# Cosine-weighted linear attention into a two-layer MLP: where one block copies v, forms k^T v and loads k, and where the last block makes four sums of g

## The chip, the cores and the metric

One core of one Trainium2 chip runs the whole program in one launch. The metric is device time of an execution in microseconds (us), the median of repeated runs. Five engines work side by side and meet at semaphores: TensorE (PE, matmuls; PEld is its weight load), VectorE (DVE), ScalarE (ACT), GpSimd (POOL) and SyncE (SP, which here only issues DMAs). A transfer moves data between HBM and SBUF, or within SBUF with a transpose; matmuls write PSUM.

## The reference

Eight batches, 8 heads, 576 rows, head dimension 64. Attention has no softmax: relu of q and k is weighted by a cosine and a sine of the row's position, which doubles the feature dimension to 128.

```python
theta = np.pi / 2.0 * pos / S
q_p = concat([relu(q) * cos, relu(q) * sin], -1)      # phi
k_p = concat([relu(k) * cos, relu(k) * sin], -1)
kv = np.einsum('bhsf,bhsd->bhfd', k_p, v)
z = np.sum(k_p, axis=2)
num = np.einsum('bhsf,bhfd->bhsd', q_p, kv)
den = np.einsum('bhsf,bhf->bhs', q_p, z)[..., None] + 1e-06
x = (num / den), heads side by side: [4608, 512]
h = x @ w_in                                          # 512 -> 2048
g = h * sigmoid(1.702 * h)
out = g @ w_out                                       # 2048 -> 512
```

## The kernel before, in words

The work goes by batch, "block b" for short: 512 rows of it in the main stream, and its last 64 rows (the tails, gathered in `xt` and `gt`) in one go with those of the other batches at the end. While PE does the two products of block b, DVE, SP and PE prepare x of block nb = b + 1, and SP loads inputs of block b + 2.

What one block needs, in the names of the code:

- q' (`trig_q`, L176): ten DVE instructions make q' in `qn` from `qf`. Five DMA transposes on SP (`qturn_dma`, L217; "turns" below) put it into `qT`. Then `load_q` (L133) refills `qf` for two blocks on, by two DMAs.
- k' (`trig`, L161, called by `kv_operands`, L877): 18 DVE instructions from `kf` into `kr`. v is copied to bf16 by `vcopy` (L187) from `vf` into `vt`, which holds a column of ones that makes the sum z along with kv.
- k^T v (`kv_mm`, L232; `kv_mm_next`, L707): 72 small matmuls on PE into a PSUM tile "at" (there are two of these); `kv_evac` (L243) copies it to `kvs` on DVE. `kv_next` (L711) does both.
- x (`x_next`, L883), chunk by chunk (four of 128 rows and one of 64): `num_mm` (L304), 8 matmuls of `qT` by `kvs` into a tile "at"; `num_div` (L315), three DVE instructions (add of epsilon, reciprocal, multiply) into `xn`; `xturn_dma` (L351), a turn on SP into `xT`.
- First product (`mm1`, L373): 16 columns blocks fc of w_in, each 4 matmuls of 512 columns (L365) and one gelu on ACT (L371) into `gT`. mm1 of a block reads all four chunks of its `xT`.
- Second product (`wino_mm`, L508): a two by two block product by seven products instead of eight (the Winograd form), p1, p2, p6, p5, p7, p3, p4 in that order, each in two column halves c of 8 matmuls of 256 columns (L519). Step s = 2p + c counts the 14 halves. It needs sums of blocks of g, s1 to s4 (`g_sums`, L466; lines L473, L475, L477, L479), each in two halves h, on DVE: s2 for p6, s1 for p5, s3 for p7, s4 for p3. s2 needs s1, and s4 needs s2. p1, p2 and p4 read g itself. `wino_after` (L566) copies a finished product aside on ACT (`keep`, L527) or joins it with a kept one on DVE (`join`, L538), and POOL issues the output's DMA (L525).

Engines run their instructions in the order in which the code writes them: the order is written out by hand, under `manual_schedule`. SP's queue is served in that order too: an SP instruction that waits for its data holds all those behind it.

For block 1 (b == 1) the order around the change is: at fc 5 (the first four column blocks are in `start_block`, L715) q' of block 2 and its turns; at fc 6 k' of block 2, then the DMAs of q of batch 3; at fc 8 the two halves of s3; at fc 12 the first halves of s1 and s2; at fc 13 v's copy; then the second halves of s1 and s2; p1 (steps 0 and 1); k^T v and its copy, the first half of s4; p2 and so on, with chunks 0 to 4 of x after steps 3, 4, 5, 6 and 8, the second half of s4 after step 6, and the loads of k and v of batch 3 (`load_kv`, L146) on SP behind the turn of chunk 3. For blocks b > 1 k^T v comes at fc 14, chunk 0 of x ahead of the second product and the others in it, and k and v are loaded behind chunk 3 likewise.

The last block (L946 on) does the tails' first product (`mm1_tails`, L393, L396), and then splits the first product of its main rows by the Winograd form too (`Unit`, L642: `step` L674, matmuls L657, adds on DVE L666, copies on ACT L671, gelu L662). Between the steps of the units, `tail_half` (L967) puts in the 14 halves of the tails' second product. Its sums (`g_sums(..., TAIL)`) go into the space of `kr` (s1, s2) and `qT` (s3, s4); those of s3 and s4 stand behind the first half. Units 0 and 1 take turns in the PSUM banks, with `Bk` common to all units, so that step 2 of a unit writes the bank that the add of the unit before has read.

Of the kernel before, what the change touches and what calls it, by code (L numbers as in the profile page):

```python
# [20 lines left out]
def kernel(  # L21
# [9 lines left out]
    nc = tc.nc  # L31
# [25 lines left out]
    def src_of(src, b, i0=0, i1=NI):  # L57
        return src[b, 2 * i0:2 * i1].rearrange("(i hh) (p j) d -> (hh p) i (j d)", hh=2, j=NS)

    qf = one.tile([128, 2560], F32, name="qf")  # L60
    kf, vf = [one.tile([128, NI, S], F32, name=n) for n in ("kf", "vf")]
# [62 lines left out]
    def load(t, src, b, eng=nc.gpsimd):  # L124
        eng.dma_start(out=t, in_=src_of(src, b))

    def load_chunks(t, src, b, eng):
        eng.dma_start(out=t[:, 0:2048].rearrange("p (h e) -> p h e", h=H),
                      in_=src[b, :, 0:512, :].rearrange("h (p c) d -> p h (c d)", c=4))
        eng.dma_start(out=t[0:64, 2048:2560].rearrange("p (h e) -> p h e", h=H),  # L130
                      in_=src[b, :, 512:S, :].rearrange("h p d -> p h d"))

    def load_q(b, eng=nc.gpsimd):  # L133
        load_chunks(qf, q, b, eng)
# [11 lines left out]
    def load_kv(b):  # L146
        load(kf, k, b, nc.sync)
        load(vf, v, b, nc.sync)
# [27 lines left out]
    def trig_q(c, act=False):  # L176
        n = 128 if c < 4 else 64
        i = chunk(qf, c)
        for cs, w in enumerate((cosw, sinw)):
            o = qn[0:n, c, :, ts(cs, 64)]  # L180
            sc = w[0:n, NS + c:NS + c + 1]
            if act:
                nc.scalar.activation(o, i, AF.Relu, scale=sc)
            else:
                nc.vector.tensor_scalar(o, i, 0.0, sc, op0=MAX, op1=MUL)  # L185

    def vcopy(i0=0, i1=NI, act=False):  # L187
        o = vt[:, :, i0:i1, 0:64].rearrange("p j i e -> p i j e")
        i = vf[:, i0:i1].rearrange("p i (j e) -> p i j e", e=64)
        if act:  # L190
            nc.scalar.activation(o, i, AF.Copy)
        else:
            nc.vector.tensor_copy(o, i)  # L193
# [23 lines left out]
    def qturn_dma(c):  # L217
        n = 128 if c < 4 else 64
        nc.sync.dma_start_transpose(out=qT[:, :, c * 128:c * 128 + n],
                                    in_=qn[0:n, c].rearrange("p h f -> p (h f)"))  # L220
# [3 lines left out]
    def kv_open(i0=0, i1=NI, n=65):  # L224
        t = pat.tile([128, 2, 512], F32, name="at")
        for i in range(i0, i1):
            st["kv", i] = t[:, :, ds((i - i0) * n, n)]
        st["ps", i0] = t[:, :, 0:(i1 - i0) * n]
        if i0 == 0:
            st["kvs"] = small.tile([128, 2, NI, VW], BF16, name="kvs", bufs=2)  # L230

    def kv_mm(i0, i1, rhs, col, n):  # L232
        for i in range(i0, i1):
            for j in range(NS):
                for hh in range(2):
                    r = slice(hh * 64, hh * 64 + 64)
                    nc.tensor.matmul(st["kv", i][:, hh, ds(col, n)], kr[r, j, i, :], rhs(r, i, j),  # L237
                                     start=(j == 0), stop=(j == NS - 1))
# [4 lines left out]
    def kv_evac(i0, i1, n=65):  # L243
        o = st["kvs"][:, :, i0:i1, 0:n]
        nc.vector.tensor_copy(o, st["ps", i0].rearrange("p hh (i e) -> p hh i e", e=n))  # L245
# [58 lines left out]
    def num_mm(c, eps_too=False):  # L304
        ps = pat.tile([128, 2, 512], F32, name="at")
        if eps_too:
            for a in range(2):
                put_eps(ps[:, a])
        for h in range(H):
            nc.tensor.matmul(ps[:, h // 4, ds((h % 4) * 65, 65)], qT[:, h, ts(c, 128)],  # L310
                             kvs_of(h), start=not eps_too,
                             stop=(not eps_too or h % 4 == 3), skip_group_check=eps_too)
        nums[c] = [ps]

    def num_div(c, eps_too=False):  # L315
        ps = nums[c][0]
        pv = ps[:, :, 0:260].rearrange("p a (h e) -> p a h e", h=4)
        den = pv[:, :, :, 64]
        if not eps_too:
            den = small.tile([128, 2, 4], F32, name="den")  # L320
            nc.vector.tensor_scalar(den, pv[:, :, :, 64], 1e-6, None, op0=ADD)  # L321
        inv = small.tile([128, 2, 4], F32, name="inv")
        nc.vector.reciprocal(inv, den)  # L323
        xn = small.tile([128, 2, 4, 64], BF16, name="xn", bufs=5)
        nc.vector.tensor_tensor(xn, pv[:, :, :, 0:64],  # L325
                                inv.unsqueeze(3).to_broadcast([128, 2, 4, 64]), op=MUL)
        nums[c].append(xn)
# [23 lines left out]
    def xturn_dma(b, c):  # L351
        xn = nums.pop(c)[1]
        n = 128 if c < 4 else 64
        nc.sync.dma_start_transpose(out=x_cols(b, c),
                                    in_=xn[0:n].rearrange("p a h e -> p (a h e)"))
# [110 lines left out]
    def g_sums(names, h, of=MAIN):  # L466

        tt = nc.vector.tensor_tensor
        a_blk, to = of
        o = {n: to[n][:, ts(h, 4)] for n in to}  # L470
        for n in names:
            if n == "s1":
                tt(o[n], a_blk(1, h), a_blk(1, h + 2), op=ADD)  # L473
            elif n == "s2":
                tt(o[n], o["s1"], a_blk(0, h), op=SUB)  # L475
            elif n == "s3":
                tt(o[n], a_blk(0, h), a_blk(1, h), op=SUB)  # L477
            else:
                tt(o[n], a_blk(0, h + 2), o["s2"], op=SUB)  # L479
# [227 lines left out]
    def kv_mm_next():  # L707
        kv_open()
        kv_mm(0, 4, vt_rhs, 0, 65)

    def kv_next():  # L711
        kv_mm_next()
        kv_evac(0, 4)
# [163 lines left out]
    def kv_operands(b):  # L877
        for j in range(NS):
            trig(kr, kf, j)
        if b > 2:  # L880
            vcopy()

    def x_next(b, c):  # L883
        num_mm(c)
        num_div(c)
        xturn_dma(b, c)


    for b in range(1, B):
        nb = b + 1 if b + 1 < B else None  # L890
        if nb is None:
            break
        f0 = 5 if b == 1 else 0
        for fc in range(f0, FC):
            if nb is not None and fc == f0:
                for c in range(5):
                    trig_q(c)
                    qturn_dma(c)
            if nb is not None and fc == f0 + 1:
                kv_operands(nb)  # L900

                if nb + 1 < B:
                    load_q(nb + 1, nc.sync)
            if fc == 8 and b == 1:
                g_sums(("s3",), 0)
                g_sums(("s3",), 1)
            if fc == 12:
                if b > 1:
                    g_sums(("s3",), 0)
                    g_sums(("s3",), 1)  # L910
                g_sums(("s1", "s2", "s4") if b > 1 else ("s1", "s2"), 0)
            if fc == 13 and b == 1:
                vcopy()
            if fc == 14 and nb is not None and b > 1:
                kv_next()
            mm1(b, fc)
        if nb is not None:
            x_open(nb)
            if b > 1:
                x_next(nb, 0)  # L920
            g_sums(("s1", "s2"), 1)
            at = ({2 * p + 1: [p + 1 if nb < B - 1 else (4, 1, 2, 3)[p]] for p in range(4)} if b > 1 else
                  {3: [0], 4: [1], 5: [2], 6: [3], 8: [4]})
            wino_open()
            for p in range(7):
                for c in range(2):
                    wino_mm(p, c)
                    s = 2 * p + c
                    if c == 1:
                        wino_after(b, p)  # L930
                    for c2 in at.get(s, ()):
                        x_next(nb, c2)
                        if c2 == 3 and nb + 1 < B:
                            load_kv(nb + 1)
                    if s == 1 and b > 1:
                        g_sums(("s4",), 1)
                    if s == 1 and b == 1:
                        kv_mm_next()
                        kv_evac(0, 4)
                        g_sums(("s4",), 0)  # L940
                    if s == 6 and b == 1:
                        g_sums(("s4",), 1)
# [3 lines left out]
    b = B - 1  # L946
# [20 lines left out]
    def tail_half():  # L967
        p, c = next(halves)
        wino_mm(p, c, TAIL)
        if c == 1:  # L970
            wino_after(None, p, end=True)
        if (p, c) == (0, 0):
            for n in ("s3", "s4"):
                for h in range(2):
                    g_sums((n,), h, TAIL)
# [73 lines left out]
```

## Time and profile before

| | us |
|---|---|
| runs shown: median (lowest to highest of 3) | 277.95 (277.95 to 279.59) |
| the profiled execution | 280.04 |
| its span in the profile | 278.2 |
| PE busy | 269.8 |
| DVE busy | 199.3 |
| ACT busy | 133.9 |
| POOL busy | 41.3 |
| first matmul of mm1 in blocks 2, 3 and 4 at | 81.04, 110.90, 139.47 |

Times in the profile are counted from the start of the span. A row of the timeline gives start, length, engine, line, operation, tiles written and read, shapes and a count; in square brackets stand the engine's idle time ahead of it and what ended that. A length of a matmul group holds the drain of its last matmul, so the next group starts before it ends. Idle time of an engine that nothing waits for costs nothing. For a DMA, the row of SP tells how long SP took to issue it; when it landed is told separately ("to landing", counted from the start of the issue). The granted clock of PE is full (1.0) throughout.

### The profile page before, as it was taken

The page shows a single profiled execution, that of the slowest core. Times are in us where ns is not written, and L with a number is a line of the kernel's source. Part 1 is how long each engine was busy: PE and PEld are TensorE (multiplying, and loading weights), DVE is VectorE, ACT ScalarE, POOL GpSimd, SP SyncE. Part 2 cuts the span into 40 slices and gives each one's busy share as a digit, 9 for nine tenths or more (in the row PEclk, how much of TensorE's full clock was granted, in tenths as well). Part 3 has the DMA queues.
Part 4 walks back from the last instruction along what each step waited for, and adds up shares of the span by engine and source line. Part 5 has one row for each costly group of instructions (what it writes and reads, how often), then busy time and mean ns, then how long its engine had stood idle before and what let it go on. Part 6 is the DMA issues. An engine that isn't in the chain of part 4 may idle for free.

```text
span 278.2 us, 6718 instructions
## 1 busy us (share of the span) xinstructions
PE 269.8 (97%) x2748; PEld 195.1 (70%) x2748; DVE 199.3 (72%) x478; ACT 133.9 (48%) x237; POOL 41.3 (15%) x70
## 2 busy tenths in 40 slices
PE   7899999999999899999999999999999999999994
PEld 2585645856975488558855895589657976899984
DVE  4943776689885986987598759876987783654741
ACT  6967642674126511652166215621563147577621
POOL 5690000000130012100110022001200162000310
PEclk9999999999999999999999999999999999999999
DMA  7999999999699999996799969988993353000233
GB/s 232 253 211 298 275 286 155 260 296 191 189 138 374 169 210 216 351 170 176 197 335 170 202 168 371 189 191 110 356 252 32 88 165 119 0 2 0 79 112 113
DMA packets 73661, 53.57 MB, mean 193 GB/s; under 512 B 52736, under 2 KB 63488, under 8 KB 73632
## 3 DMA queue, kind: packets, MB, share of 16 engines
q1 hardware_dynamic: 67504, 36.97, 59.8%
q0 software_dynamic: 6128, 16.19, 21.2%
q8 instruction: 21, 0.34, 0.5%
q14 instruction: 8, 0.07, 0.1%
HBM read 36.70 MB, written 9.44 MB: 166 GB/s over the span
## 4 chain that ended last, share of the span: by engine, by line
PE 77%; DVE 10%; DMA 9%; SPq 1%; issue 1%; ACT 1%
PE mm L519 29%; PE mm L365 25%; DMA kf<-in_k_dram 9%; PE mm L396 4%; DVE kr L169 4%; PE mm L421 4%; PE mm L657 4%; PE at L519 3%; PE at L237 3%; PE at L310 3%; DVE vt L193 1%; DVE sums L477 1%; PE mm L205 1%; PE mm L388 1%; DVE sums L475 1%
## 5 line engine op out<-in xcount | busy, mean ns | idle before, releaser
L365 PE MATMUL mm<-xT,w_in 128*128 128x512 bf16 (+1 forms) x528 | 99.8, 345 | 0.0
L371 ACT ACTIVATE g<-mm 128x512 bf16<-128x512 f32 x112 | 66.0, 598 | 35.0 <-PE mm L365 35.0
L365 PEld LDWEIGHTS <-w_in 128*128 128x128 bf16 x528 | 53.0, 113 | 40.3
L519 PEld LDWEIGHTS <-sums 128*128 128x128 bf16 x448 | 42.4, 98 | 4.7
L525 POOL DMA_DIRECT2D out_dram<-ysb x24 | 17.4, 725 | 184.9 <-DVE inv L323 75.0
L519 PE MATMUL mm<-wsum,sums 128*128 128x256 bf16 x336 | 40.1, 272 | 0.0
L519 PEld LDWEIGHTS <-g 128*128 128x128 bf16 x336 | 32.1, 98 | 3.8
L169 DVE TENSOR_SCALAR kr<-kf,cosw 128x256 bf16<-128x256 f32 x69 | 24.4, 354 | 9.2 <-DMA kf<-in_k_dram 9.2
L325 DVE TENSOR_TENSOR xn<-at,inv 128x512 bf16<-128x512 f32 x39 | 27.0, 691 | 1.4
L519 PE MATMUL mm<-w_out_sb,g 128*128 128x256 bf16 x224 | 26.6, 273 | 0.0
L169 DVE TENSOR_SCALAR kr<-kf,sinw 128x256 bf16<-128x256 f32 x68 | 23.3, 342 | 0.0
L185 DVE TENSOR_SCALAR qn<-qf,cosw 128x512 bf16<-128x512 f32 (+1 forms) x33 | 16.4, 498 | 2.9 <-DMA qf<-in_q_dram 2.9
L534 ACT ACTIVATE kept_p<-mm 128x512 f32<-128x512 f32 (+1 forms) x15 | 8.5, 569 | 19.8 <-PE mm L519 19.8
L586 ACT ACTIVATE ysb<-mm 128x512 f32<-128x512 f32 x6 | 3.6, 598 | 29.0 <-PE mm L519 29.0
L310 PEld LDWEIGHTS <-qT 128*128 128x128 bf16 x312 | 14.3, 97 | 3.3 <-issue 1.0
L310 PE MATMUL at<-kvs,qT 128*128 128x65 bf16 x312 | 15.7, 193 | 0.8 <-DVE kvs L245 0.8
L321 DVE TENSOR_SCALAR den<-at 128x8 f32<-128x8 f32 x36 | 5.9, 163 | 14.7 <-PE at L310 14.6
L534 ACT ACTIVATE kept_u<-mm 128x512 f32<-128x512 f32 (+1 forms) x8 | 4.3, 544 | 24.9 <-DVE xn L325 16.8
L185 DVE TENSOR_SCALAR qn<-qf,sinw 128x512 bf16<-128x512 f32 (+1 forms) x33 | 15.7, 475 | 0.0
L421 PE MATMUL mm<-w_out_sb,g 128*128 128x512 bf16 x64 | 14.8, 379 | 0.0
L519 PE MATMUL mm<-w_out_sb,sums 128*128 128x256 bf16 x112 | 13.4, 273 | 0.0
L519 PE MATMUL mm<-wsum,g 128*128 128x256 bf16 x112 | 13.4, 272 | 0.0
(147 smaller groups left out, 320.2 us busy)
## 6 DMA issues: line engine op xcount, KB each, us to landing
kf<-in_k_dram SPq DMA_DIRECT2D x6, 1152.0 KB, 6.5
vf<-in_v_dram SPq DMA_DIRECT2D x6, 1152.0 KB, 11.2
qf<-in_q_dram SPq DMA_DIRECT2D x6, 1024.0 KB, 6.7
out_dram<-ysb POOLq DMA_DIRECT2D x24, 256.0 KB, 6.5
w_out_sb<-in_moe_w_out_dram POOLq DMA_DIRECT2D x4, 512.0 KB, 17.6
kf<-in_k_dram POOLq DMA_DIRECT2D x1, 1152.0 KB, 13.2
vf<-in_v_dram POOLq DMA_DIRECT2D x1, 1152.0 KB, 20.8
w_in<-in_moe_w_in_dram POOLq DMA_DIRECT2D x2, 512.0 KB, 10.0
```

What stands on the lines that cost most here:

```text
L169: eng.tensor_scalar(o, i, 0.0, w[:, j:j + 1], op0=MAX, op1=MUL)
L185: nc.vector.tensor_scalar(o, i, 0.0, sc, op0=MAX, op1=MUL)
L310: nc.tensor.matmul(ps[:, h // 4, ds((h % 4) * 65, 65)], qT[:, h, ts(c, 128)], kvs_of(h), start=not eps_too, stop=(not eps_too or h % 4 == ...
L325: nc.vector.tensor_tensor(xn, pv[:, :, :, 0:64], inv.unsqueeze(3).to_broadcast([128, 2, 4, 64]), op=MUL)
L365: nc.tensor.matmul(hp[fc][:, t0:t1], wcol(kc, fc), x[b][:, kc, t0:t1], start=(kc == 0), stop=(kc == KC - 1))
L371: nc.scalar.activation(gT[fc // 4][:, fc % 4], hp.pop(fc), AF.Gelu_apprx_sigmoid)
L396: nc.tensor.matmul(hps[:, 64:B * 64], wcol(kc, fc), xt[:, kc, 64:B * 64], start=(kc == 0), stop=(kc == KC - 1))
L421: nc.tensor.matmul(yp[b, t, c0][:, c0:c1], w, w_out_sb[:, fc, c0:c1], start=(fc == 0), stop=(fc == FC - 1))
L519: nc.tensor.matmul(bank[to][c], lhs, rhs, start=opens, stop=(fc == HF - 1), skip_group_check=True)
L525: eng.dma_start(out=dst[:, 2 * i + c0:2 * i + c1, ts(n, HD)], in_=t[:, c0:c1])
L534: nc.scalar.activation(o, i, AF.Identity)
L657: nc.tensor.matmul(to[:, j], lhs, rhs, start=(opens and j == 0 and k == 0), stop=(k == 1), skip_group_check=True)
```

## The change

In block 1 alone: v's copy goes from fc 13 to fc 8, where s3 stood, right behind k'. k^T v goes from behind p1 to ahead of the second product, and its copy behind the second halves of s1 and s2. The halves of s3 go behind that copy and behind step 2 (after chunk 0 of x), those of s4 behind steps 4 and 6. Chunks 0, 1 and 2 of x come after steps 2, 3 and 4 instead of 3, 4 and 5; chunks 3 and 4 stay at 6 and 8. On SP, k of batch 3 is loaded ahead of q of batch 3, where it was loaded behind the turn of chunk 3; v of batch 3 stays there.

In the last block: the four DVE instructions for s3 and s4 of the tails come after the second `tail_half` instead of the first, and so behind the first add of unit 0 (step 2, `c11`).

No instruction is added or taken away on any engine, as the order of the instructions on each engine shows: only places change.

```diff
@@ -900,17 +900,16 @@
                 kv_operands(nb)
 
                 if nb + 1 < B:
+                    if b == 1:
+                        load(kf, k, nb + 1, nc.sync)
                     load_q(nb + 1, nc.sync)
             if fc == 8 and b == 1:
-                g_sums(("s3",), 0)
-                g_sums(("s3",), 1)
+                vcopy()
             if fc == 12:
                 if b > 1:
                     g_sums(("s3",), 0)
                     g_sums(("s3",), 1)
                 g_sums(("s1", "s2", "s4") if b > 1 else ("s1", "s2"), 0)
-            if fc == 13 and b == 1:
-                vcopy()
             if fc == 14 and nb is not None and b > 1:
                 kv_next()
             mm1(b, fc)
@@ -918,9 +917,14 @@
             x_open(nb)
             if b > 1:
                 x_next(nb, 0)
+            else:
+                kv_mm_next()
             g_sums(("s1", "s2"), 1)
+            if b == 1:
+                kv_evac(0, 4)
+                g_sums(("s3",), 0)
             at = ({2 * p + 1: [p + 1 if nb < B - 1 else (4, 1, 2, 3)[p]] for p in range(4)} if b > 1 else
-                  {3: [0], 4: [1], 5: [2], 6: [3], 8: [4]})
+                  {2: [0], 3: [1], 4: [2], 6: [3], 8: [4]})
             wino_open()
             for p in range(7):
                 for c in range(2):
@@ -931,12 +935,14 @@
                     for c2 in at.get(s, ()):
                         x_next(nb, c2)
                         if c2 == 3 and nb + 1 < B:
-                            load_kv(nb + 1)
+                            if b > 1:
+                                load(kf, k, nb + 1, nc.sync)
+                            load(vf, v, nb + 1, nc.sync)
                     if s == 1 and b > 1:
                         g_sums(("s4",), 1)
-                    if s == 1 and b == 1:
-                        kv_mm_next()
-                        kv_evac(0, 4)
+                    if s == 2 and b == 1:
+                        g_sums(("s3",), 1)
+                    if s == 4 and b == 1:
                         g_sums(("s4",), 0)
                     if s == 6 and b == 1:
                         g_sums(("s4",), 1)
@@ -969,7 +975,7 @@
         wino_mm(p, c, TAIL)
         if c == 1:
             wino_after(None, p, end=True)
-        if (p, c) == (0, 0):
+        if (p, c) == (0, 1):
             for n in ("s3", "s4"):
                 for h in range(2):
                     g_sums((n,), h, TAIL)
```

## The prediction

> **What bounds the kernel now.** I read the page's first part, then the waits of TensorE (PE), the chain that ended last, and the timeline around each wait. The page says that PE is the bound:
>
> ```profile
> PE 269.8 (97%) x2748; PEld 195.1 (70%) x2748; DVE 199.3 (72%) x478; ACT 133.9 (48%) x237; POOL 41.3 (15%) x70
> ```
>
> Only some 8 us of the span are PE idle, so the change can win no more than the waits it removes. Of the waits of PE (total, times, longest) three lie where it works:
>
> ```profile
> PE at L237 <- DVE vt L193: 0.9, 2, 0.5
> PE at L310 <- DVE kvs L245: 0.8, 1, 0.8
> PE mm L657 <- DVE qn L666: 0.3, 1, 0.3
> ```
>
> The timeline (start, length, engine, line) puts them at four places:
>
> ```profile
> 64.19 1.29 DVE L477 TENSOR_TENSOR sums<-g 128x1024 bf16<-128x1024 bf16 x2
> ...
> 65.68 1.91 PE L519 MATMUL mm<-w_out_sb,g 128*128 128x256 bf16 x16
> ...
> 66.73 1.35 DVE L193 CAST vt<-vf 128x2304 bf16<-128x2304 f32 x1
> ...
> 68.14 1.26 PE L237 MATMUL at<-vt,kr 64*128 64x65 bf16 x72 [0.55 <-DVE vt L193]
> 69.33 1.92 PE L519 MATMUL mm<-w_out_sb,g 128*128 128x256 bf16 x16
> ...
> 87.46 0.35 DVE L169 TENSOR_SCALAR kr<-kf,cosw 128x256 bf16<-128x256 f32 x1 [3.20 <-DMA kf<-in_k_dram]
> ...
> 93.60 1.26 PE L237 MATMUL at<-vt,kr 64*128 64x65 bf16 x72 [0.31 <-DVE vt L193]
> ...
> 97.47 0.40 PE L310 MATMUL at<-kvs,qT 128*128 128x65 bf16 x8 [0.76 <-DVE kvs L245]
> ...
> 239.39 1.28 DVE L477 TENSOR_TENSOR qT<-gt 128x1024 bf16<-128x1024 bf16 x2
> ...
> 241.79 0.68 DVE L666 TENSOR_TENSOR qn<-qn,mm 128x512 f32<-128x512 f32 x1
> ...
> 242.53 0.60 PE L657 MATMUL mm<-xT,w_in 128*128 128x256 bf16 x4 [0.29 <-DVE qn L666]
> ```
>
> In block 1, k^T v waits for the copy of v, which stands behind four sums. In block 2, VectorE (DVE) idles 3.20 us for k(3) (k of batch 3) and is then late for k^T v and for its copy to kvs. In the last block the add that frees a PSUM bank stands behind four sums. The queue of SyncE (SP) is the last view:
>
> ```profile
> 66.27 0.57 SPq L128 DMA_DIRECT2D qf<-in_q_dram  x1
> 66.90 0.63 SPq L130 DMA_DIRECT2D qf<-in_q_dram  x1
> ...
> 77.05 1.73 SPq L354 DMA_TRANSPOSE xT<-xn  x1
> 78.83 0.58 SPq L125 DMA_DIRECT2D kf<-in_k_dram  x1
> 79.46 0.49 SPq L125 DMA_DIRECT2D vf<-in_v_dram  x1
> ...
> 81.76 5.82 SPq L219 DMA_TRANSPOSE qT<-qn  x1
> ...
> 156.20 1.20 SPq L354 DMA_TRANSPOSE xT<-xn  x1
> ```
>
> k(3) is issued only at 78.83, after the fourth turn (DMA transpose) of x, and lands 8.6 us later. A turn issued while loads are in flight can hold SP for 5.82 us, or for the usual 1.2.
>
> **The change, part by part.** No arithmetic is added: PE and DVE run the same instructions in another order, and SP issues the same DMAs. All is made against the profiled execution (280.04 us, span 278.2, 1.84 around it). The median of the runs is 277.95, 2.09 below it; I take the savings over unchanged.
>
> *Block 1, v's copy and k^T v.* The copy moves from behind four sums to 64.19, right behind k'. v(2) landed at 50.23 + 12.1 = 62.3, so it need not wait, and ends at 64.19 + 1.27 = 65.46. PE leaves mm1 for the second product at 65.68, so k^T v starts there with 0.2 to spare. Before, PE did 16 matmuls (1.76, as from 69.33 to the next group at 71.09), stood until 68.14, then k^T v (1.19). Now 65.68 + 1.19 + 1.76 = 68.63 stands against 69.33: minus 0.70. The next mm1, of block 2, then opens at 81.04 - 0.70 = 80.34.
>
> What is queued on DVE behind the copy: s1 and s2 (0.72 and 0.61 a half) end at 66.8 and 68.1, the second half needing the gelu that ends at 66.5; kvs 68.1 to 68.7, wanted by PE at 69.5; s3's first half 69.3. With 1.04 for each division (den, inv, xn) and 0.61 for each further sum or join, in the order of the instructions, xn of chunks 0 to 3 end near 71.1, 73.4, 74.4 and 76.1, and s4's halves at 75.0 and 76.6. The second half of s4 is wanted at 77.3 (p3, fifth matmul) and s3 at 74.9. Cover: 0.7 and 3 us; if it were gone PE would stand for what is missing.
>
> *The turns of x, the open cost.* q(3) and now k(3) ahead of it are in SP's queue when xn of chunk 0 is ready at 71.1. k(3) is issued at 66.27 without a wait (kf is last read at 64.5) and delays q(3)'s issue by 0.63. k lands 6.3 us after issue where nothing is ahead (the load at 106.40), so near 72.6; a second load of that size landed 2.9 (v after k, at 62.3), 3.2 or 5.1 us behind, so q(3) at 75.5 to 77.7, wanted by DVE at 79.4: covered. The turns stand behind both. Before, they went at 73.11, with q landed at 72.6, and the fourth at 77.05 landed 3.2 later, at 80.25, only 0.8 ahead of mm1. Now the fourth is ready at 76.1. If SP is free, it lands 2.5 to 4.1 us later (rows of xT), 78.6 to 80.2, and costs nothing. The other end: turn 0 held until q lands at 77.7, turn 1 for 3.07 (the qT row at 87.68), two of 1.25 more: turn 3 at 82.1, landed at 85.3, PE standing 4.9. The nearest row is the turn at 156.20: also x, also behind a running q load, 1.20 on SP, landed after 4.3. I go by it: turn 3 issued by about 76.5, landed by 79.9, cost 0.
> The Trainium skill ("DMA: Bandwidth & Descriptors", section "Queues, rings and completion order") says that each DMA engine consumes one queue's descriptors in ring order, which speaks against this change: turns can't overtake k and q. By that alone the sum would be rival B's 276.5, by the row 275.5; the trace agrees as far as 4.3 us to landing behind a load against 2.5 without shows.
>
> *Block 2, k(3) early.* Blocks 3 and 4 open their first mm1 at 110.90 and 139.47, 28.57 apart; block 2 takes 81.04 to 110.90, 29.86. The excess, 1.29, is the two waits. With k(3) in at 72.6, DVE goes from the q work (end 84.2, now 83.5) straight to k', done 4.73 later at 88.3, and v's copy next. v(3) is issued right after turn 3, near 77.9, with no k ahead: 6.3 to 11.2 us to landing, 84 to 89. At the late end copy and five sums (1.27 + 0.61 x 5 + 0.1) end at 93.5, kvs at 94.2, for PE's 97.47 - 0.70 - 1.29 = 95.5: covered, by 1.3. Minus 1.29, down to minus 1.0 if v is as late as 90.7, as before.
>
> *Last block, the sums.* PE ends a group of four at 241.64 + 0.44 = 242.08 and starts at 242.53: 0.45 lost. With s3 and s4 of the tail (four of 0.60) behind the add, the add runs at 239.4 as its operand is there (matmul from 238.59), the sums end at 242.4, and the next add wants its operand at 242.6. s3 is read at 252.57. Minus 0.45, or 0 if another wait takes over.
>
> **Sum.** 0.70 + 1.29 + 0.45 = 2.44: the profiled execution 277.6 (span 275.8), the median 275.5, 0.9% less. The waits of profile and median may differ by some tenths, as the 2.09 between them shows that waits do shift: 275.0 to 275.9 for this case.
>
> **Rivals.**
> B: *the turns come late, the gain of block 1 is eaten.* SP is held in turn 0 until q lands at 75.5; turns 1 and 2 take 1.27 each, so that turn 3 starts at 78.0 and lands 3.2 later at 81.2. PE, which wants it at 80.34, stands 0.9: 276.4 to 276.5, and between 275.9 and 277.0 as q lands some tenths earlier or later. For it: SP was held for 5.82 us at 81.76, and for 2.17 in the x turn at 127.63, both with loads in flight; against: 1.20 at 156.20.
> C: *slower.* The same place, but turn 1 is held too (3.07): turn 1 ends at 78.6, turn 2 at 79.9, turn 3 lands at 83.1, PE stands 2.8 and more than the whole gain of 2.44 is gone: 278.3, and up to 280.4 with q at 77.7. It decides from a landing later than 80.34 + 2.44 = 82.8. Against: two long holds in a row stand only in rows of qT, with twice the data of xT.
> The Trainium skill ("Perfetto Trace Analysis", section "DMA Instruction — HWDGE (DVE, Sync)") states that the issuing slice runs until all descriptors are generated, and that these can fill a buffer; the 5.82 agrees, and whether two loads fill it for x's turns no row shows.
> D: *k(3) early does not pay.* Something else, v(3) or the sums, is what PE waits for in block 2: 277.95 - 0.70 - 0.45 = 276.8. Against: blocks 3 and 4 run the same chain without a wait.
>
> **How the numbers follow.** Forecast 0.60, B 0.21, D 0.11, C 0.08. Predicted 275.5. The range 275.0 to 277.0 holds the forecast, B and D but for their edges, and leaves out C. About 1% is what a measurement here tells from no change: 275.17 and 280.73. Faster 0.10 (the lower sixth of the forecast's own range), slower 0.02 (C's upper end), same 0.88.
>
> **What would show it.** Block 1: k^T v directly behind mm1 without a wait, mm1 of block 2 opening near 80.3; if turns are late, an idle there put down to a DMA of xT. Block 2: no DVE wait for kf, no PE wait at L237 and L310, 28.6 us from mm1 to mm1. Tail: no PE wait at L657. I am wrong if mm1 of block 2 opens after 81.0, or block 2 stays above 29 us.

## The result, and the profile after

The changed kernel takes 277.62 us, the median of 22 runs (277.31 to 278.54). The kernel before, in 22 runs beside them, takes 278.82 (277.95 to 280.21). The ratio is 0.996, 95% interval 0.9949 to 0.9971: 1.2 us faster, where 2.44 was forecast. The median that the prediction subtracted from, 277.95, was of three runs, two of which are the fastest of its 22.

The profiled execution of the changed kernel took 277.36 us, span 275.6. Its page and the list of PE's waits:

```profile
PE 269.3 (98%) x2748; PEld 195.0 (71%) x2748; DVE 199.4 (72%) x478; ACT 133.9 (49%) x237; POOL 41.3 (15%) x70
```

```profile
PE mm L699 <- DVE wsum L81: 1.2, 1, 1.2
PE mm L251 <- DVE kr L169: 0.6, 1, 0.6
PE mm L299 <- DVE xh L291: 0.2, 1, 0.2
```

L237, L310 and L657 are gone from the list; what is left lies in the first 15 us, ahead of all that was changed. The same places in the timeline:

```profile
55.90 9.66 PE L365 MATMUL mm<-xT,w_in 128*128 128x512 bf16 x44
...
62.53 1.34 DVE L193 CAST vt<-vf 128x2304 bf16<-128x2304 f32 x1
...
65.36 0.52 SPq L125 DMA_DIRECT2D kf<-in_k_dram  x1
...
65.49 1.26 PE L237 MATMUL at<-vt,kr 64*128 64x65 bf16 x72
...
75.92 1.22 SPq L354 DMA_TRANSPOSE xT<-xn  x1
...
78.39 1.91 PE L519 MATMUL mm<-wsum,g 128*128 128x256 bf16 x16
80.22 12.25 PE L365 MATMUL mm<-xT,w_in 128*128 128x512 bf16 x56
...
108.79 12.25 PE L365 MATMUL mm<-xT,w_in 128*128 128x512 bf16 x56
```

k^T v (65.49) follows mm1 without a bracket of idle time; mm1 of block 2 opens at 80.22 and that of block 3 at 108.79, 28.57 later, which is also what blocks 3 and 4 of the kernel before are apart. The first row belongs to mm1 of block 1. In the profile before it reads

```profile
56.18 9.66 PE L365 MATMUL mm<-xT,w_in 128*128 128x512 bf16 x44
```

so the changed kernel's execution was 0.28 us ahead at that point, before anything that was changed. Of the 0.82 by which mm1 of block 2 opens earlier (81.04 before), 0.54 were won in block 1. And the fourth turn of x, issued at 75.92, lands at 80.18, 0.04 ahead of mm1: from k^T v to mm1 of block 2 takes 14.73 here, 14.64 in the second profile of the changed kernel (at the end of the experiments), where the turn landed earlier. PE stood some 0.09 for it, too short for a bracket. In the last block:

```profile
237.27 0.68 DVE L666 TENSOR_TENSOR qn<-qn,mm 128x512 f32<-128x512 f32 x1
237.87 1.28 DVE L477 TENSOR_TENSOR qT<-gt 128x1024 bf16<-128x1024 bf16 x2
```

The add now stands ahead of the sums, and PE goes through. So the three waits are gone from this profile, as the prediction said. That its span comes so near (275.6 against 275.8) is partly luck: it is 2.6 shorter than before, and 0.28 of that lies ahead of block 1; the waits gave 0.54, 1.29 and 0.45. What has to be explained is why taking away these waits moved the median by 1.2 only.

### The profile page after: what moved, and what is told of

It is laid out like the page before. It is cut to its first block, busy times and chain, and to the rows that moved or that the text cites. A ratio compares the mean times of both kernels' runs of the same rounds, so it can differ in the third digit from the quotient of the medians.

```text
span 275.6 us, 6720 instructions
## 1 busy us (share of the span) xinstructions
PE 269.3 (98%) x2748; PEld 195.0 (71%) x2748; DVE 199.4 (72%) x478; ACT 133.9 (49%) x237; POOL 41.3 (15%) x70
## 4 chain that ended last, share of the span: by engine, by line
PE 93%; DMA 4%; DVE 1%; ACT 0%; issue 0%; POOL 0%
PE mm L365 35%; PE mm L519 31%; PE mm L421 5%; PE mm L657 4%; PE at L519 4%; PE mm L396 4%; PE at L237 4%; PE at L310 3%; DMA sums<-in_v_dram 2%; DMA kf<-in_k_dram 1%; PE at L342 1%; PE mm L388 1%; DVE xn L325 1%; PE mm L205 0%; ACT xT L349 0%
## 5 line engine op out<-in xcount | busy, mean ns | idle before, releaser
L310 PEld LDWEIGHTS <-qT 128*128 128x128 bf16 x312 | 14.3, 97 | 2.4
L310 PE MATMUL at<-kvs,qT 128*128 128x65 bf16 x312 | 15.7, 193 | 0.0
```

## The experiments

Two theories. Theory 1: the waits in blocks 1 and 2 hang on when two loads land, which differs from one execution of the same program to the next; the profiled execution of the kernel before was one with late landings, and only the wait of the last block is there every time. Theory 2: the waits are constant, and the changed kernel has a new wait (for the turns of x) in most executions, which its profiled one escaped.

**The kernel before, twice more** (no edit; the first with a ratio of 1.0004, 0.9991 to 1.0017).

> The kernel before, unchanged. Theory 1: of the three waits that the change removes, only the tail's 0.45 us stands in every execution; those of block 1 (0.70) and block 2 (1.29) hang on when k(2) and k(3) land, which was late in the execution first profiled (280.04 us, against a median of 278.82 over 22 runs). Then this profile, if its time is near the median, shows them smaller: less than 1.1 us of PE idle at L237 and L310 together, span near 277. Theory 2: the waits are the same in every execution; then 0.55, 0.31 and 0.76 us again, and the missing gain lies in a wait of the changed kernel that its profiled execution escaped. Ratio 1.000 either way.

> The kernel before a third time, for its profile alone. Theory 1: the waits of blocks 1 and 2 have other sizes again (0 to 0.7 and 0 to 1.3 us), growing with the landing of k(2) and k(3); the tail's 0.45 is the same.

The first took 278.75 us in its profiled execution, span 276.9, the second 279.14, span 277.3. The rows of DVE's wait for k(3) and of PE's waits behind it, of the first:

```profile
67.95 1.26 PE L237 MATMUL at<-vt,kr 64*128 64x65 bf16 x72 [0.65 <-DVE vt L193]
...
86.18 0.35 DVE L169 TENSOR_SCALAR kr<-kf,cosw 128x256 bf16<-128x256 f32 x1 [2.10 <-DMA kf<-in_k_dram]
...
241.25 0.60 PE L657 MATMUL mm<-xT,w_in 128*128 128x256 bf16 x4 [0.29 <-DVE qn L666]
```

and of the second:

```profile
67.68 1.26 PE L237 MATMUL at<-vt,kr 64*128 64x65 bf16 x72
...
86.56 0.35 DVE L169 TENSOR_SCALAR kr<-kf,cosw 128x256 bf16<-128x256 f32 x1 [2.76 <-DMA kf<-in_k_dram]
...
96.56 0.40 PE L310 MATMUL at<-kvs,qT 128*128 128x65 bf16 x8 [0.70 <-DVE kvs L245]
...
241.62 0.60 PE L657 MATMUL mm<-xT,w_in 128*128 128x256 bf16 x4 [0.29 <-DVE qn L666]
```

Same instructions, other waits. The 0.29 (0.45 from start to start) in the last block is in all three; the block 1 wait is missing in one; block 2 stands for L237 and L310 in one, for L310 alone in another, for neither by 0.15 us or more in the third. Laid out, with block 1's loss counted from start to start (its 16 matmuls take 1.76; 0.09 passes there without a wait too), block 2's as its length less 28.57, and in the last columns the start of the row of mm1 of block 1 shown above and what is left without it:

| kernel before, execution of | block 1 | block 2 | last block | the time less the three | mm1 of block 1 at | less that too |
|---|---|---|---|---|---|---|
| 280.04 us | 0.61 | 1.29 | 0.45 | 277.69 | 56.18 | 221.51 |
| 278.75 us | 0.70 | 0.20 | 0.45 | 277.40 | 55.90 | 221.50 |
| 279.14 us | 0 | 0.86 | 0.45 | 277.83 | 56.34 | 221.49 |

Less its own waits, each execution falls into the range of the changed kernel's runs, 277.31 to 278.54. The last column is the same in all three: the three waits and the start of block 1 are the whole difference between these executions. k(2) landed at 59.44 and 59.27 where block 1 waits, and at 57.64 where it doesn't. That is what theory 1 says, and it goes against the constant waits of theory 2. My estimate that the waits at L237 and L310 would come to less than 1.1 us of idle held in both (0.65 and 0.70).

**The last block alone.**

```diff
-        if (p, c) == (0, 0):
+        if (p, c) == (0, 1):
             for n in ("s3", "s4"):
```

> Only the edit of the last block. Both theories: minus 0.45 us, ratio 0.9984, no PE wait at L657 and those of blocks 1 and 2 as in the kernel before. By theory 1 this is the one constant part of the gain.

Ratio 0.9983 (0.9966 to 1.0), the wait at L657 gone: as both expected, 0.5 us, though the interval by itself reaches no change. Its profiled execution (277.62 us) happened to have no PE wait in block 1 or 2 either, with the old order and k(3) late in the queue:

```profile
65.23 1.35 DVE L193 CAST vt<-vf 128x2304 bf16<-128x2304 f32 x1
...
85.31 0.35 DVE L169 TENSOR_SCALAR kr<-kf,cosw 128x256 bf16<-128x256 f32 x1 [1.76 <-DMA kf<-in_k_dram]
```

So an idle DVE ahead of block 3's k' costs PE nothing up to about 1.8 us. Over the seven profiles in which k(3) is loaded late, those of the runs below among them (DVE's wait: length of block 2 over 28.57), it reads 1.12: 0; 1.39: 0; 1.76: 0; 2.10: 0.20; 2.76: 0.86; 2.83: 0.93; 3.20: 1.29. Past a slack of 1.9 us it is one for one.

**Block 1's order alone, and k(3) early alone.** The first is the change without its SP part and without the last block; the second is this:

```diff
                 if nb + 1 < B:
+                    if b == 1:
+                        load(kf, k, nb + 1, nc.sync)
                     load_q(nb + 1, nc.sync)
...
-                            load_kv(nb + 1)
+                            if b > 1:
+                                load(kf, k, nb + 1, nc.sync)
+                            load(vf, v, nb + 1, nc.sync)
```

> Only block 1's order on PE and DVE (copy of v, k^T v, sums, chunks of x), with k(3) loaded as before and the last block as before. Theory 1: between 0 and minus 0.5 us, as the wait for the copy of v is small where k(2) lands earlier. Theory 2: minus 0.70 us, ratio 0.9975. Block 2 keeps its wait for k(3) in both.

> Only k(3) ahead of q(3) on SP. Theory 1: minus 0.3 to 0.9 us. Theory 2: minus 1.29 us, ratio 0.9954. In both no DVE wait for kf ahead of block 3's k', and block 2 takes 28.6 us from mm1 to mm1. If the turns of x then land late, PE stands ahead of mm1 of block 2, by up to 0.9.

Measured: 0.9991 (0.9974 to 1.0008) and 0.9992 (0.9976 to 1.0007). Neither can be told from no change by itself. The second is 0.2 us, less than the 0.3 to 0.9 expected by theory 1, though its interval reaches them. Theory 2's 0.9954 for k(3) lies outside the interval; theory 2's 0.9975 for the order lies at its edge. With the last block's 0.9983 the three points multiply to 0.9966, beside the 0.996 of the whole. Their profiles had no PE wait in blocks 1 and 2: in the first DVE waited 1.39 us for k(3), under the slack; in the second the copy of v came at 65.02, in the old order, and PE had no wait for it.

**k(2) made to land late**, by loading v(2) ahead of it, in the kernel before and with block 1's new order alone:

```diff
-    load_kv(2)
+    load(vf, v, 2, nc.sync)
+    load(kf, k, 2, nc.sync)
```

> The kernel before with v(2) loaded ahead of k(2), so that k(2) lands some 3 us later in every execution. Theory 1 (block 1's wait is the lateness of k(2)): k' of block 2 then ends near 66, the copy of v 3.8 later, and PE, which wants it at 67.4, waits 1.5 to 3.5 us at L237 in block 1 in every execution; 1.5 to 2.5 us slower than before. Theory 2 (the wait is that of the order alone): still 0.55 to 0.65, ratio 1.000.

> The same late k(2), with block 1's new order on PE and DVE, k(3) and the last block as before. Theory 1: the copy of v now follows k' by 1.27 us instead of 3.8, and PE wants it 1.75 earlier, so the wait at L237 is 0.8 us shorter than in the run with the old order: what the order is worth once k(2) is late. Theory 2: 0.70 faster than the kernel before.

The old order: 1.0118 (1.0069 to 1.0168), the new: 1.0062 (1.0035 to 1.009). k(2) landed 12.0 and 12.6 us after its issue, where it took 8.1 to 10.0 in the runs with the loads as before. The rows of the old order:

```profile
61.14 0.35 DVE L169 TENSOR_SCALAR kr<-kf,cosw 128x256 bf16<-128x256 f32 x1 [3.13 <-DMA kf<-in_k_dram]
68.41 1.36 DVE L193 CAST vt<-vf 128x2304 bf16<-128x2304 f32 x1
69.82 1.26 PE L237 MATMUL at<-vt,kr 64*128 64x65 bf16 x72 [2.37 <-DVE vt L193]
```

The wait at L237 grew to 2.37 as k(2) came later, which theory 2 has no place for. The 3.3 us lost are more than the 1.5 to 2.5 expected; part of them is lost clock, of which more below. With k(2) late, the old order is behind the new by 0.0056, 1.6 us, where 0.8 was expected. The two intervals overlap, so the size is open, and the direction is likely rather than shown. The profiles can't settle it: the one of the new order had a still later k(2) (k' from 62.88), a wait of 3.29 and then PE at half its clock.

**k(3) on another queue.**

```diff
-                        load(kf, k, nb + 1, nc.sync)
+                        load(kf, k, nb + 1)
```

> The changed kernel, with k(3) issued by GpSimd instead of SP, so that it doesn't stand ahead of the turns of x. In the changed kernel's profile the fourth turn, issued at 75.92, landed at 80.22, just when mm1 of block 2 opened: no slack. Theory 1: the changed kernel rarely waits there, so this is equal within 0.1 us, with the fourth turn landing near 79. Theory 2 (a new wait for the turns of x in most executions eats the gain): 0.5 to 1 us faster than the changed kernel, ratio to before near 0.993.

0.9966 (0.9946 to 0.9987): the changed kernel's own 0.996, and not theory 2's 0.993. The landing that I expected near 79 was wrong: the fourth turn was issued at 76.50 and landed 4.35 us later, at 80.84, and mm1 opened only then, at 80.98, in an execution that was 0.67 late at k^T v (66.16). From k^T v to mm1 it took 14.82, 0.18 over the 14.64: PE stood for the turn here too. So the 4.3 is not made by k(3) standing in SP's queue; k(3) and q(3) were in flight all the same.

**More ahead of the turns.** In a first form v(3)'s load stands between k(3) and q(3), which is ahead of the copy of v(2) in program order; the copy then takes v of batch 3 for block 2, and waits for it.

> The changed kernel with v(3) too ahead of q(3) on SP. 1.15 MB more stands ahead of the turns of x, some 3 us. Both theories: the fourth turn lands near 82 to 83, PE stands 1.5 to 3 us ahead of mm1 of block 2 and the kernel is slower than before. If it isn't, the turns have slack that the profile doesn't show.

1.04 (1.0361 to 1.044), PE standing 10.4 us for the copy: it says nothing on the turns. In a second form v(3) and q(3) are loaded behind the copy:

```diff
                     if b == 1:
                         load(kf, k, nb + 1, nc.sync)
-                    load_q(nb + 1, nc.sync)
+                    else:
+                        load_q(nb + 1, nc.sync)
             if fc == 8 and b == 1:
                 vcopy()
+                load(vf, v, nb + 1, nc.sync)
+                load_q(nb + 1, nc.sync)
...
                             if b > 1:
                                 load(kf, k, nb + 1, nc.sync)
-                            load(vf, v, nb + 1, nc.sync)
+                                load(vf, v, nb + 1, nc.sync)
```

> The changed kernel with k(3), v(3) and q(3) in that order on SP, v(3) and q(3) issued behind the copy of v(2), which here keeps its data. 1.15 MB more than in the changed kernel stands ahead of the turns of x, some 3 us. If the turns have no slack, the fourth lands near 82 to 83 and PE stands 1.5 to 3 us ahead of mm1 of block 2; ratio 1.001 to 1.006. If they have slack, no such wait and ratio 0.996.

1.0198 (1.0174 to 1.0223), worse than expected. SP and PE in its profile:

```profile
66.54 0.51 SPq L128 DMA_DIRECT2D qf<-in_q_dram  x1
67.10 4.46 SPq L130 DMA_DIRECT2D qf<-in_q_dram  x1
71.66 10.72 SPq L354 DMA_TRANSPOSE xT<-xn  x4
```

```profile
PE mm L365 <- DMA xT<-xn: 6.4, 1, 6.4
```

SP is held 4.46 us in q's second part, 3.92 in turn 0 and 2.77 in turn 1; turn 3 lands at 86.8 and PE stands 6.4 us, and then works for some 3 us at half its clock. That is the mechanism of rival C (turns 0 and 1 held, turn 3 late), with a hold in q's own issue besides, and with three loads ahead instead of two: the changed kernel stands one load away from it.

**The changed kernel again.**

> The changed kernel again. Theory 1: ratio 0.996 as before; its profile shows no PE wait in blocks 1 and 2 and in the last block, and span differences to 275.6 come from ahead of block 1. Theory 2: in an execution above the median (277.6), PE stands ahead of mm1 of block 2 for the fourth turn of x by 0.3 us or more.

0.9954 (0.9936 to 0.9971), span 275.7, no PE wait in blocks 1 and 2 or the last block; the fourth turn landed at 79.8, mm1 opened at 80.36. The profiled execution (277.64) was not above the median by enough to test theory 2's half of this expectation. So the constant waits of theory 2 are refuted; of its new wait the three profiles that have the changed kernel's order and k(3) early show 0.09, 0.18 (k(3) on GpSimd) and 0 us. What the slower executions of the changed kernel (up to 278.54) lose, and where, was not profiled.

## Why the prediction was wrong, point by point

- *What bounds the kernel, and the three waits*: right. All were where it put them, and all are gone.
- *Block 1, minus 0.70 and mm1 of block 2 at 80.34*: the mechanism held; that 80.22 is so near is luck by the 0.28 that lie ahead of block 1. In its own execution the term was 0.61, as 0.09 pass between the two products without a wait too. And the size was that of one execution: 0.61, 0.70 and 0 in three, and none in the profiles of the last block alone and of k(3) early alone.
- *The turns of x, cost 0*: nearly right, with a slip in the sum. By the row that I went by, a turn issued at 76.5 that lands after 4.3 lands at 80.8 and not at 79.9, and would have cost 0.5 against 80.34. Turn 3 was issued at 75.92 and landed after 4.3, at 80.18; the cost was 0.09, and 0.18 where it was issued at 76.50. There was no cover. Rivals B and C did not happen: what B had wrong is that SP would be held in turn 0 until q lands. SP issued turn 0 in 1.47 us while k and q were in flight, and turn 0 then landed at 76.71, 0.44 behind the second part of q. The Trainium skill ("DMA: Bandwidth & Descriptors", section "Queues, rings and completion order") has the descriptors of one queue consumed in ring order on each DMA engine; that order of landing agrees with it, and B's 276.5 did not follow from it. The hold came one load further on (6.4 us of standing).
- *Block 2, minus 1.29*: the mechanism held (28.57), the size was that of one execution: 1.29, 0.20 and 0.86. The bound "down to minus 1.0" was set by v(3)'s landing; nothing bounded it by k(3)'s own, though the median landing on the page of the profile (6.5 us) stood beside the 8.6 of this load. Rival D's 276.8 came nearer to the 277.62, but not by its reason: nothing else held PE in block 2 (28.57 with k(3) early alone, too), the wait itself was smaller.
- *Last block, minus 0.45*: right, and the same in every execution profiled with the old order there.
- *The step that failed*: "The median of the runs is 277.95, 2.09 below it; I take the savings over unchanged." The savings came from an execution of 280.04, the base from one of 277.95. Made against its own execution the sum said 277.6, and 277.36 (the profile, 0.28 of it from ahead of the change) and 277.62 (the median) were measured. By the table an execution without the three waits takes 277.4 to 277.8, so one of 277.95 holds 0.1 to 0.6 of them, hardly more than the last block's 0.45, and not 2.44. Against the medians, 275.5 is 2.1 too low: 0.87 of that is the base (277.95 of three runs, 278.82 of 22), 1.24 the savings (2.44, where 1.2 was measured). The bound on this step, "some tenths", should have been as wide as the 2.09 itself. The signs by which I would be wrong (mm1 of block 2 after 81.0, block 2 above 29 us) looked at the mechanism alone, and so could not show it.

For an execution at the median the three terms are then 0.45, and by subtraction some 0.75 together for blocks 1 and 2 (1.2 less 0.45; the two alone gave 0.25 and 0.2), where the prediction had 1.99.

## What to carry to other kernels

Subtract what a profile shows from that execution's own time, and hold the result against the fastest runs shown: a forecast far below them, made of waits that a fast run may not have, is to be doubted before it is tried. A wait that a DMA ends is not a constant: find its slack (here 1.9 us of DVE idle) and count only what lies beyond it in a typical execution, by more than one profile if there are any. Here the change narrowed the spread as well as moving the median: 277.31 to 278.54 after, 277.95 to 280.21 before. And look where the profiled execution stood ahead of the change, before its times behind it are taken for a gain.

## What the runs showed of the hardware that was not expected

The same load of 1152 KB from the same place of the program landed after 8.6, 7.1 and 7.7 us (k(3), kernel before), and after 6.9 and 6.7 in two kernels that are the same up to there but for block 1's order or nothing at all. What makes the difference was not tried.

PE lost half its clock in the longest waits. With k(2) late and the new order it stood 3.29 us, until 69.02; the columns are the window, its length, busy time of PE, PEld, DVE, ACT and POOL, then the granted clock, the DMA engines' share and GB/s:

```profile
69.00:73.00 4.00, 3.98 (x81) 3.35 (x81) 3.76 (x6) 0.00 (x0) 0.00 (x0) 0.50 0.89 279
73.00:77.00 4.00, 4.00 (x43) 3.33 (x41) 1.02 (x4) 0.60 (x1) 0.00 (x0) 0.79 0.02 5
77.00:81.00 4.00, 4.00 (x50) 3.63 (x49) 3.85 (x11) 0.60 (x1) 0.71 (x1) 1.00 0.45 116
```

The granted clock is 0.50 for 5.7 us after the wait, which costs about 2.6 more: mm1 opens 17.27 us after k^T v, against 14.64 in the run with the new order and k(2) as before. It had fallen 2.1 us into this wait, and 2.5 and 2.8 us into those of 6.4 us (more ahead of the turns, second form) and 10.4 us (first form). After the wait of 2.37 in the old order it stayed at 1.00; but of the six runs of that kernel, three at 281.2 to 281.3 us have a mean clock of 1.0, and three at 283.1 to 285.8 us one of 0.985 to 0.994. The Trainium skill ("TensorE: Matmul & The Clock Gate", section "What's actually happening") gives the throttled state after at least one idle window of about 3.4 us, in windows that run freely. Here the clock fell sooner, and the measurement decides.
